# Attention's list schedule: spacings, transposes and exclusions in the planner's costs, and two bias blocks recorded behind the q/k scale's broadcast

## The chip, the cores and the metric

The kernel runs on one core of a Trainium2 chip. The metric is the device time of one execution in microseconds (us). The engines are TensorE (PE, with its weight loads as PEld), VectorE (DVE), ScalarE (ACT), GpSimd (POOL) and SyncE (SP), whose queue issues the DMAs.

## What is computed

An attention with a learned relative bias, whose output is the input of a mixture of experts with a Sinkhorn gate:

```python
# q, k, v: 4 x 8 heads x 576 x 64
scores = q @ k.T / 8
x = log1p(|i - j|) / log1p(max(i, 1))           # 576 x 576
bias = relu(x @ w1 + b1) @ w2                    # one plane for each head
attn = softmax(scores + bias)
y = (attn @ v)                                   # 2304 tokens x 512
P = exp(y @ w_gate - max); 8 times: rows / sum, columns / sum, * N / E
out = sum over 8 experts of P[:, e] * (relu(y @ w1[e]) @ w2[e])     # 512 -> 1024 -> 512
```

## The kernel before, in words

The program has two parts, and each is written to one `Plan`: the code records instructions with an engine, a cost in us, the regions that they read and write, and a priority, and `emit` then orders them. This change concerns the first part, attention, which in the profiled execution takes the first 490 us.

**Attention.** There are 16 units (a batch and a pair of heads). A unit has five steps: two query groups for each head with two tiles of 128 queries each, and one step with a single tile. A step takes for each tile: score matmuls on PE into a PSUM tile (`s`, two buffers), one fused DVE instruction that adds the bias and finds the row's extreme (`sb`, the custom instruction), an exponential with its sum on ACT (in place in `sb`), a scaled copy to 16 bits on ACT (`ah`, high part), and a DVE instruction for the low part. One DMA transpose per step then brings `ah` (18 blocks of 128x128, or 9 for a single tile) into `aT`, and two steps later `attend` multiplies it with the values (28 matmuls into `pv`), after which ACT and DVE split `pv` into two 16-bit parts in the buffers `xa`, `xb`, `xc`. `ah` has two buffers, and a third in `xc` for a part of the units. Besides, each unit has loads of q, k, v and bias, a split of q and k into 16-bit parts (`u_cut`), 18 PE transposes (`u_trans`) and some copies on POOL (`pairs`). PE fills its free time with pieces of expert 0 (`run_piece`, recorded with the lowest priority), whose results go through ACT and POOL.

**Before the first unit** the maxima of q and k are found (loads of 576 KB, one reduction each on DVE or ACT), and their bias is built in 41 blocks. `bias_step` number i records `bias_front(i)` (four matmuls into PSUM tiles `pv`, `l1`, `l2`, `l1`, a Sign on ACT behind each, and the load of a later block's input) and `bias_back(i-1)` (34 or fewer matmuls into `s`, and two or three DVE instructions). The tag `l2` has one PSUM buffer, and the broadcast of the q/k maximum (`bcast_max`: a transpose on PE, a reduction, a diagonal, a matmul, a copy) uses the same buffer twice. Its result `s_qk` is what `u_cut(0)` waits for; bias blocks from number 18 on need the scale as well.

**The order.** `emit` simulates the engines: each has a time at which it is free, each recorded instruction a time at which its inputs are ready (the end of the producer plus `LATENCY` of the pair of engines), and each engine takes at its turn the ready instruction of the lowest priority number and, within one, of the lowest record number; an instruction of priority 0 that is about to be ready holds others back. DMAs go through one pipe (`moved`). The instructions are then emitted in the order of their simulated starts, so what reaches the chip is an order per engine, and waits of an engine in that order hold up all that stands behind. Costs come from `Engine.cost` and `Engine.transfer`, which look at sizes and memory spaces. The second part (gate, Sinkhorn, experts) has costs written beside each instruction; it shares the table `LATENCY` alone.

Old costs of the lines concerned: an exponential over 576 columns is put at 0.16 + 0.03 + 576 x 0.00097 + 0.28 us (the last term for `accum_out`), a transpose DMA at 0.65 us on SP and 2.97 us in the pipe for 18 blocks.

Of the kernel before, what the change touches and what calls it, by code (L numbers as in the profile page):

```python
# [10 lines left out]
F32 = mybir.dt.float32  # L11
# [4 lines left out]
PSUM = bass.MemoryType.PSUM  # L16
DRAM = bass.MemoryType.DRAM

P = 128
# [16 lines left out]
SK = 3.0  # L36
PC = 1.305
MXP = 2
K_VEC = (1, 4, 7)
TM16 = 2.0**-16  # L40
TINY = 2.0**-100


class Plan:
# [1 line left out]


    LATENCY = {
        ("act", "act"): 0.13,
        ("dve", "dve"): 0.13,  # L50
        ("pool", "pool"): 0.1,
        ("pe", "pe"): 0.0,
        ("sp", "sp"): 0.0,
        ("dve", "pe"): 0.26,
        ("pe", "act"): 0.2,
        ("pe", "dve"): 0.2,
    }

    def record(self, eng, cost, fn, ins, outs, move=None):
# [71 lines left out]
    def emit(self):  # L131
        n = self.nodes
        succ, left, ready = [[] for _ in n], [len(x[3]) for x in n], [0.0] * len(n)
        for i, x in enumerate(n):
            for d in x[3]:
                succ[d].append(i)
        avail = {}
        for i, x in enumerate(n):
            if not left[i]:
                avail.setdefault(x[0], []).append(i)  # L140
        free, order, moved = {}, [], 0.0
        key = lambda i: (n[i][4], i)

        def pick(e):

            l = avail[e]
            t = max(free.get(e, 0.0), min(ready[i] for i in l))
            for i in sorted((i for i in l if ready[i] <= t), key=key):
                if not any(n[j][4] == 0 and n[i][4] and t < ready[j] < t + n[i][1] - 0.25 for j in l):
                    return t, e, i  # L150
            t = min(ready[j] for j in l if ready[j] > t)
            return t, e, min((i for i in l if ready[i] <= t), key=key)

        while any(avail.values()):
            t, e, i = min(pick(e) for e in avail if avail[e])
            avail[e].remove(i)
            order.append((t, i))
            free[e] = end = t + n[i][1]
            if n[i][6]:
                moved = max(moved, end + 0.65) + n[i][6][0]  # L160
                end = moved + 0.8
                if e == "dma":
                    free[e] = max(free[e], moved - n[i][6][1])
            for j in succ[i]:
                left[j] -= 1
                ready[j] = max(ready[j], end + n[i][5] + self.LATENCY.get((e, n[j][0]), 0.17))
                if not left[j]:
                    avail.setdefault(n[j][0], []).append(j)
        assert len(order) == len(n)
        for _, i in sorted(order):  # L170
            n[i][2]()
        self.__init__()
# [17 lines left out]
class Engine:  # L190
# [5 lines left out]
    def __getattr__(self, op):  # L196
        def call(*args, **kw):
            outs = [kw[k] for k in ("out", "accum_out") if k in kw]
            rest = list(args)
            if "out" not in kw:  # L200
                outs.insert(0, rest.pop(0))
            ins = [x for x in rest + [v for k, v in kw.items() if k not in ("out", "accum_out")] if isinstance(x, AP)]
            if op == "matmul" and not kw["start"]:
                ins.append(outs[0])
            fn = getattr(self.real, op)
            move = None
            if op.startswith("dma"):
                cost, *move = self.transfer(op, outs[0], ins[0])
            else:
                cost = self.cost(op, outs[0], ins) + (0.28 if self.name == "act" and len(outs) > 1 else 0.0)  # L210
            self.plan.record(self.name, cost, lambda: fn(*args, **kw), ins, outs, move)  # L211

        return call

    def transfer(self, op, out, src):

        if op == "dma_start_transpose":
            return 0.65, 0.165 * out.free_size() / P, 0.92
        run = 1
        for step, n in reversed(list((src if src.space == DRAM else out).ap)):  # L220
            if step != run:
                break
            run *= n
        slow = 2.0 if run * mybir.dt.size(out.dtype) < 512 else 1.0
        return 1.05 if self.name == "pool" else 0.5, out.nbytes() / 275e3 * slow, 1.25

    def cost(self, op, out, ins):

        n = max(x.free_size() for x in [out] + ins)
        columns = sum(x.free_size() == 1 for x in ins)  # L230
        if self.name == "pe":
            c = 4 if ins[0].dtype == F32 else 1
            if out.partition_size() > 64:
                return c * max(64, out.free_size()) / 2350
            return c * max(82, out.free_size()) / 3500
        if self.name == "act":
            return (0.13 if ins and ins[0].space == PSUM else 0.16) + 0.03 * columns + n * 0.00097
        if self.name == "pool":
            return 0.15 + n * (0.0016 if len(ins) - columns < 2 else 0.0021)
        if op == "tensor_copy" and ins[0].dtype == out.dtype == F16:  # L240
            return 0.06 + n * 0.00027
        if n <= 2:
            return 0.08
        return 0.12 + n * (0.0012 if ins[0].space != PSUM else 0.00112)


class Places:
# [24 lines left out]
def attention_sinkhorn_moe(ctx, tc, q, k, v, w1, b1, w2, wg, m1, m2, xm, xm4, xf, sel, out):  # L272
# [12 lines left out]
    vec, act, pool, pe, sync = (  # L285
        Engine(plan, e, n)
        for e, n in ((nc.vector, "dve"), (nc.scalar, "act"), (nc.gpsimd, "pool"), (nc.tensor, "pe"), (nc.sync, "dma"))
    )
# [126 lines left out]
    with ExitStack() as actx:  # L415
# [108 lines left out]
        for kind in range(1, 4):  # L524
            vec.scalar_tensor_tensor(
                out=wr,
# [101 lines left out]
        def bias_step(between=()):  # L628

            i = bpos[0]  # L630
            bpos[0] += 1
            if between:
                if 0 < i <= NBLK:
                    bias_back(i - 1)
                for j, fn in enumerate(between):
                    fn()
                    if j == 0 and i < NBLK:
                        bias_front(i)
                return
            if i < NBLK:  # L640
                bias_front(i)
            if 0 < i <= NBLK:
                bias_back(i - 1)
# [153 lines left out]
        for n in range(8):  # L797
            for m in (2 * n, 2 * n + 1):
                nm, _, i = qk_order[m]
                some_max(mq8[:, int(nm == "k"), i : i + 1], mxt.pop((nm, i)), nm == "k" and i not in K_VEC)  # L800
                if m + 4 < 16:
                    max_load(*qk_order[m + 4])
                elif m + 4 == 16:
                    u_load(0)
                if m + 4 >= 16:
                    max_load("v", v, m - 12)
            bias_step()
            bias_step()
        with plan.urgent():
            mqk = sm([P, 2])  # L810
            vec.tensor_reduce(out=mqk, in_=mq8, axis=AX.X, op=ALU.max)
# [12 lines left out]
            out=g, in0=g0, scalar=s_qk[:, 0:1], in1=s_qk[:, 1:2], op0=ALU.mult, op1=ALU.mult  # L824
        )
        gbox[0] = g[:, 0:1]
        bias_step()

        def b_scale(hp):

# [21 lines left out]
            u_trans(0)  # L852
        u_load(1)
        u_cut(1)
        bias_step()
        b_scale(0)
        u_trans(1)

# [1142 lines left out]
```

## Time and profile before

| what | value |
|---|---|
| median of 3 runs | 1739.29 us (1737.27 to 1740.19) |
| the profiled execution's own time | 1741.8 us |
| its span, first to last instruction | 1740.0 us |
| PE, DVE, ACT, POOL busy | 1666.5, 1437.2, 1057.8, 149.3 us |
| TensorE clock granted, mean | 0.986 of full speed |

The profile is of one execution. Busy time is the union of an engine's instructions; a share of the whole span mixes the attention part, where all engines work, with the expert part, where PE does nearly all of it. The two parts are therefore read in stretches of their own.

### The profile page before, as it was taken

The numbers are of one execution on the slowest core, as the hardware profiler recorded it, in microseconds if no ns is written. First come the engines' busy times: TensorE is split into PE (matmuls) and PEld (weight loads), VectorE is DVE, ScalarE is ACT, GpSimd is POOL, SyncE is SP. The second block draws the span as 40 slices with busy tenths as digits, with TensorE's granted clock in tenths as the row PEclk, the third lists the DMA queues.
The fourth block names the chain that finished last, engine by engine and source line by source line (L and its number), as shares of the span: only waits on it lengthen the run. The fifth ranks groups of instructions, "written<-read, shape, count | busy, mean of one in ns | idle before, by whom it ended". The sixth has DMA issues, their size and how long they took to land.

```text
span 1740.0 us, 40362 instructions
## 1 busy us (share of the span) xinstructions
PE 1666.5 (96%) x16596; PEld 1367.8 (79%) x16596; DVE 1437.2 (83%) x2595; ACT 1057.8 (61%) x1879; POOL 149.3 (9%) x191
## 2 busy tenths in 40 slices
PE   7887897999999999999999999999999999999998
PEld 4554564656585888888988898889888888888887
DVE  7998999889769999687878887988788878876666
ACT  7887888888857555456455545555555644443443
POOL 0102231323212300000000000000000000000000
PEclk9988898999999999999999999999999999999999
DMA  7869999999875446644664555456544743462321
GB/s 256 257 174 233 186 205 216 212 213 213 177 239 200 158 161 239 232 150 143 217 231 170 176 190 209 176 178 238 203 165 159 279 157 131 183 225 97 102 75 37
DMA packets 291964, 324.60 MB, mean 187 GB/s; under 512 B 183100, under 2 KB 217412, under 8 KB 286788
## 3 DMA queue, kind: packets, MB, share of 16 engines
q1 hardware_dynamic: 291780, 322.04, 61.6%
q8 instruction: 129, 2.11, 0.5%
q14 instruction: 55, 0.45, 0.1%
HBM read 191.43 MB, written 88.08 MB: 161 GB/s over the span
## 4 chain that ended last, share of the span: by engine, by line
PE 76%; DVE 5%; DMA 2%; ACT 1%; issue 1%; POOL 0%; DVEq 0%; SPq 0%; ACTq 0%; POOLq 0%
PE bankA L1612 18%; PE bankA L1632 14%; PE bankE L1632 9%; PE bankB L1632 9%; PE bankE L1612 9%; PE l L211 6%; PE bankB L1612 4%; PE pv L211 3%; PE s L211 2%; DMA aT<-ah 1%; PE bankB L375 1%; DVE c L1224 1%; DMA xb<-in_moe_w_dram 1%; PE bankE L375 1%; DVE ah L211 0%
## 5 line engine op out<-in xcount | busy, mean ns | idle before, releaser
L1612 PEld LDWEIGHTS <-slot 128*128 128x128 f16 x5040 | 451.0, 98 | 52.2 <-issue 6.4
L1632 PEld LDWEIGHTS <-hA 128*128 128x128 f16 x2268 | 221.0, 98 | 26.6 <-DVE hA L1224 1.2
L211 PEld LDWEIGHTS <-area 128*128 128x128 f16 (+1 forms) x2477 | 153.6, 100 | 101.3 <-issue 31.7
L1612 PE MATMUL bankA<-xt,slot 128*128 128x256 f16 (+1 forms) x1680 | 186.1, 262 | 1.4 <-ACT u L1669 1.4
L1612 PE MATMUL bankE<-xt,slot 128*128 128x256 f16 (+1 forms) x1680 | 186.1, 262 | 0.3 <-DVE c L1224 0.3
L1657 ACT ACTIVATE hA<-c 128x512 f16<-128x512 f32 x189 | 118.3, 628 | 107.8 <-DVE c L1224 106.8
L1632 PEld LDWEIGHTS <-hS 128*128 128x128 f16 x1512 | 147.6, 98 | 20.2 <-DVE hS L1663 1.9
L1632 PEld LDWEIGHTS <-area 128*128 128x128 f16 x1512 | 147.7, 98 | 17.1
L1716 ACT COPY u<-bankA 128x512 f32<-128x512 f32 (+1 forms) x70 | 38.0, 542 | 181.3 <-PE bankA L1632 181.2
L1224 DVE SCALAR_TENSOR_TENSOR hA<-c,hA 128x512 f16<-128x512 f32 x189 | 128.4, 691 | 15.9 <-ACT hA L1657 13.9
L1669 ACT ACTIVATE u<-bankA 128x512 f32<-128x512 f32 x126 | 75.2, 597 | 79.0 <-PE bankA L1612 72.2
L211 ACT ACTIVATE sb<-sb,st 128x576 f32<-128x576 f32 x144 | 110.5, 769 | 8.7 <-DVE st L211 8.5
L211 PE MATMUL l<-area 128*128 128x512 f16 (+1 forms) x413 | 110.6, 384 | 4.7 <-ACT area L211 1.3
L211 DVE SCALAR_TENSOR_TENSOR ah<-sb,st,ah 128x576 f16<-128x576 f32 x121 | 101.8, 869 | 13.4 <-ACT ah L211 12.9
L1224 DVE SCALAR_TENSOR_TENSOR acc<-c,fs,acc 128x256 f32<-128x256 f32 x252 | 110.3, 479 | 2.1
L211 ACT ACTIVATE ah<-sb,st 128x576 f16<-128x576 f32 x121 | 88.5, 770 | 19.3 <-DMA aT<-ah 14.4
L211 PE MATMUL s<-qkT 128*128 128x512 f16 (+3 forms) x560 | 82.7, 296 | 16.1 <-DVE st L211 14.7
L1632 PE MATMUL bankA<-area,hS 128*128 128x256 f16 x756 | 88.9, 273 | 1.8 <-ACT hS L1657 1.0
L1632 PE MATMUL bankA<-area,hA 128*128 128x256 f16 x756 | 88.4, 273 | 1.0 <-DVE hA L1224 1.0
L1632 PE MATMUL bankB<-area,hA 128*128 128x256 f16 x756 | 88.3, 273 | 0.0
L1632 PE MATMUL bankB<-area 128*128 128x256 f16 x756 | 88.3, 273 | 0.0
L1632 PE MATMUL bankA<-area 128*128 128x256 f16 x756 | 88.3, 273 | 0.0
(248 smaller groups left out, 3192.2 us busy)
## 6 DMA issues: line engine op xcount, KB each, us to landing
sc_w<-stage SPq DMA_DIRECT2D x84, 512.0 KB
acc<-sc_y SPq DMA_DIRECT2D x102, 256.0 KB
area<-sc_w SPq DMA_DIRECT2D x48, 512.0 KB
sc_y<-acc SPq DMA_DIRECT2D x84, 256.0 KB
xt<-sc_t SPq DMA_DIRECT2D x20, 1024.0 KB
slot<-sc_w SPq DMA_DIRECT2D x36, 512.0 KB
bt<-sc_bias SPq DMA_DIRECT2D x26, 576.0 KB
raw<-in_moe_w_dram SPq DMA_DIRECT2D x28, 512.0 KB
```

Source lines behind the costliest of these rows:

```text
L211: self.plan.record(self.name, cost, lambda: fn(*args, **kw), ins, outs, move)
L375: pe.matmul(ps, w[:, a, ft * P : (ft + 1) * P], xs(xp, dt, p0, W), start=(dt == 0 and j == 0), stop=(dt == 3 and j == 2),)
L1224: vec.scalar_tensor_tensor(out=o, in0=x, scalar=s, in1=y, op0=op0, op1=op1)
L1612: pe.matmul(ps[:, jf * w : jf * w + w], t[:, a, c * 512 + f * P : c * 512 + f * P + P], x(xp, c), start=(first and jf == 0 and c == 0 and ...
L1632: pe.matmul(ps[:, j * 256 : j * 256 + 256], h[:, a, fc * w + j * P : fc * w + j * P + P], t[:, wp, fc * 256 : fc * 256 + 256], start=(firs ...
L1657: on_act(0.58, lambda: act.activation(h[:, 0, sl], x, AF.Relu if relu else AF.Copy), [r], wk)
L1669: on_act(0.55, lambda: act.activation(tmp[k], bank[b], f, scale=HS), [b], [k], 0)
L1716: on_act(0.27 * nt, lambda: act.copy(tmp[k][:, :n], bank[b][:, :n]), [b], [k], 0)
```

## The change

`LATENCY`, the costs of all engines, the handling of DMAs and the simulation of transposes are replaced; a rule is added that POOL instructions and DVE instructions with several SBUF inputs (or with one, where copies and `tensor_scalar` are concerned) don't run at once; and the two `bias_step`s that the last round of the maxima recorded (numbers 15 and 16) are recorded after the q/k scale. The next two follow `u_cut(1)`, where before one stood ahead of `u_cut(0)` and one behind `u_cut(1)`. What is computed, and the instructions themselves, stay.

```diff
+EARLY = 2
+PEC = 1.08
     LATENCY = {
-        ("act", "act"): 0.13,
-        ("dve", "dve"): 0.13,
-        ("pool", "pool"): 0.1,
+        ("act", "act"): 0.055,
+        ("act", "dve"): 0.225,
+        ("act", "pe"): 0.225,
+        ("dve", "dve"): 0.06,
+        ("dve", "act"): 0.2,
+        ("dve", "pe"): 0.2,
+        ("pool", "pool"): 0.0,
+        ("pool", "dve"): 0.12,
+        ("pool", "pe"): 0.12,
         ("pe", "pe"): 0.0,
+        ("pe", "act"): 0.29,
+        ("pe", "dve"): 0.29,
         ("sp", "sp"): 0.0,
-        ("dve", "pe"): 0.26,
-        ("pe", "act"): 0.2,
-        ("pe", "dve"): 0.2,
     }
...
             order.append((t, i))
+            if e == "pool" or n[i][6] == "shared":
+                t = max(t, free.get(("shared", e != "pool"), 0.0))
+                free["shared", e == "pool"] = t + n[i][1]
             free[e] = end = t + n[i][1]
-            if n[i][6]:
-                moved = max(moved, end + 0.65) + n[i][6][0]
-                end = moved + 0.8
-                if e == "dma":
-                    free[e] = max(free[e], moved - n[i][6][1])
+            if n[i][6] and n[i][6] != "shared":
+                if not n[i][6][0]:
+                    free[e] = end = max(end, moved - 0.2 + n[i][1])
+                moved = max(moved, end + 0.5) + n[i][6][0]
+                end = moved + 0.75
+                free[e] = max(free[e], moved - n[i][6][0] - n[i][6][1]) if n[i][6][0] else free[e]
...
+            big = [x for x in ins if x.free_size() > 1]
+            if self.name == "dve" and not any(x.space == PSUM for x in big):
+                one = len(big) == 1 and op in ("tensor_scalar", "tensor_copy", "tensor_single_scalar")
+                move = "shared" if len(big) > 1 or one and outs[0].free_size() > 1 else None
...
-                cost = self.cost(op, outs[0], ins) + (0.28 if self.name == "act" and len(outs) > 1 else 0.0)
+                cost = self.cost(op, outs[0], ins) + (0.093 if self.name == "act" and len(outs) > 1 else 0.0)
...
         if op == "dma_start_transpose":
-            return 0.65, 0.165 * out.free_size() / P, 0.92
+            return 0.149 * out.free_size() / P + 0.06, 0.0, 0.0
...
-        return 1.05 if self.name == "pool" else 0.5, out.nbytes() / 275e3 * slow, 1.25
+        return 0.5, out.nbytes() / 300e3 * slow, 1.5
...
         if self.name == "pe":
-            c = 4 if ins[0].dtype == F32 else 1
-            if out.partition_size() > 64:
-                return c * max(64, out.free_size()) / 2350
-            return c * max(82, out.free_size()) / 3500
+            c = (4 if ins[0].dtype == F32 else 1) * max(64, out.free_size()) / 2375
+            return PEC * (c if out.partition_size() > 64 else c / 2)
         if self.name == "act":
-            return (0.13 if ins and ins[0].space == PSUM else 0.16) + 0.03 * columns + n * 0.00097
+            return (0.052 if psum else 0.186) + n * 0.00083
         if self.name == "pool":
-            return 0.15 + n * (0.0016 if len(ins) - columns < 2 else 0.0021)
+            return 0.08 + n * (0.00115 if len(full) < 2 else 0.0025)
+        if op == "tensor_tensor_reduce":
+            return 0.735
+        if n <= 2:
+            return 0.183 if op.startswith("tensor_s") else 0.165 if op == "tensor_copy" else 0.09
         if op == "tensor_copy" and ins[0].dtype == out.dtype == F16:
-            return 0.06 + n * 0.00027
-        if n <= 2:
-            return 0.08
-        return 0.12 + n * (0.0012 if ins[0].space != PSUM else 0.00112)
+            return 0.6 if psum else 0.16 + n * 0.00027
+        if op == "tensor_scalar" and not psum:
+            return 0.12 + n * 0.00054
+        return 0.065 + n * 0.00106 + (0.055 if len(full) > 1 and op == "scalar_tensor_tensor" else 0.0)
...
-            bias_step()
-            bias_step()
+            if n < 7:
+                bias_step()
+                bias_step()
         with plan.urgent():
             mqk = sm([P, 2])
...
         gbox[0] = g[:, 0:1]
-        bias_step()
+        for _ in range(EARLY):
+            bias_step()
...
         u_cut(1)
-        bias_step()
+        for _ in range(4 - EARLY):
+            bias_step()
         b_scale(0)
```

## Rows read from the trace of the kernel before

**Rows 1.** Stretches: us, busy PE PEld DVE ACT POOL (count), clock, DMA share, GB/s

```profile
60.00:150.00 90.00, 78.32 (x1079) 48.45 (x1076) 83.80 (x167) 80.89 (x160) 15.76 (x27) 0.94 0.74 196
150.00:300.00 150.00, 122.45 (x1188) 75.99 (x1187) 138.39 (x312) 120.60 (x238) 35.21 (x47) 0.91 0.97 211
300.00:450.00 150.00, 143.32 (x1452) 93.80 (x1453) 131.98 (x299) 125.43 (x256) 44.85 (x58) 0.98 1.05 215
...
700.00:1740.00 1040.00, 1031.45 (x9908) 926.46 (x9905) 819.15 (x1339) 530.98 (x877) 0.00 (x0) 1.00 0.49 171
```

**Rows 2.** Timeline, all engines, near 490: start us, us, engine, line, what

```profile
490.81 1.36 PE L1280 MATMUL bankS<-wgs,xa 128*128 128x8 f16 x48
```

**Rows 3.** Groups by form, 0 to 490: names, shapes, count | busy us, mean ns

```profile
L211 ACT ACTIVATE sb<-sb,st 128x576 f32<-128x576 f32 x144 | 110.5, 769 | 8.7 <-DVE st L211 8.5
...
L211 ACT ACTIVATE area<-l 128x512 f16<-128x512 f32 x120 | 65.0, 625 | 4.4 <-PE l L211 4.2
```

**Rows 4.** Timeline, ACT and DVE: starts of like instructions one behind the other

```profile
53.65 1.57 ACT L211 ACTIVATE area<-l 128x512 f16<-128x512 f32 x3
...
307.43 0.76 ACT L211 ACTIVATE sb<-sb,st 128x576 f32<-128x576 f32 x1
...
308.18 0.77 ACT L211 ACTIVATE sb<-sb,st 128x576 f32<-128x576 f32 x1
...
311.76 0.81 DVE L211 CUSTOM_DVE_ANT_0 sb<-s,bt,sms 128x576 f32<-128x576 f32 x1
...
312.50 0.81 DVE L211 CUSTOM_DVE_ANT_0 sb<-s,bt,sms 128x576 f32<-128x576 f32 x1
```

**Rows 5.** Who waited for whom, 0 to 490: us in total, times, longest us

```profile
PE s L211 <- DVE st L211: 17.9, 18, 3.0
...
ACT ah L211 <- DMA aT<-ah: 14.4, 13, 2.6
DVE ah L211 <- ACT ah L211: 12.9, 13, 2.6
DVE sb L211 <- PE s L211: 11.8, 16, 1.9
...
DVE xc L211 <- ACT xc L211: 5.9, 3, 4.5
DVE aT L211 <- PE s L211: 5.5, 9, 1.1
...
PE pv L211 <- DMA aT<-ah: 4.2, 5, 1.9
```

**Rows 6.** Timeline, all engines: from the q/k maximum to the first cut

```profile
47.11 0.17 DVE L211 TENSOR_REDUCE sms<-sms 128x2 f32<-128x16 f32 x1
...
48.22 1.73 ACT L211 ACTIVATE area<-l 128x512 f16<-128x512 f32 x3
...
55.24 0.27 PE L211 MATMUL l<-ident,sms 128*2 128x128 f32 x1
...
59.35 1.44 ACT L211 ACTIVATE qk<-nat,sms 128x576 f16<-128x576 f32 x2
```

**Rows 7.** Chain of waits in order of time: start us, us, what

```profile
311.52 1.89 PE pv L211 x28
...
393.57 5.04 DMA aT<-ah
```

**Rows 8.** Timeline, SP's queue: the transpose of the chain above

```profile
393.57 3.10 SPq L211 DMA_TRANSPOSE aT<-ah  x1
```

**Rows 9.** Instructions by tile `aT`: duration ns min/median/max, first and last start us

```profile
L211 SPq DMA_TRANSPOSE aT<-ah x67: 1277/3104/5950, 91.6 to 483.5; - x67
...
L211 SPq DMA_TRANSPOSE aT<-xc x13: 1277/2110/4824, 232.5 to 390.3; - x13
```

**Rows 10.** Timeline, all engines: a POOL copy and a DVE scaling of resident bias

```profile
64.19 1.80 POOL L211 COPY qkT<-qkT 64x576 uint32<-64x576 uint32 x2 [61.66 <-ACT qkT L211]
64.20 1.26 DVE L211 TENSOR_SCALAR br<-br,sms 128x1152 f32<-128x1152 f32 x1
```

More of the change, by code (lines that the diff above doesn't have):

```diff
@@ L224, in transfer @@
         slow = 2.0 if run * mybir.dt.size(out.dtype) < 512 else 1.0
-        return 1.05 if self.name == "pool" else 0.5, out.nbytes() / 275e3 * slow, 1.25
+        return 0.5, out.nbytes() / 300e3 * slow, 1.5
     def cost(self, op, out, ins):
         n = max(x.free_size() for x in [out] + ins)
-        columns = sum(x.free_size() == 1 for x in ins)
+        full = [x for x in ins if x.free_size() > 1]
+        psum = any(x.space == PSUM for x in full)
         if self.name == "pe":
-            c = 4 if ins[0].dtype == F32 else 1
-            if out.partition_size() > 64:
-                return c * max(64, out.free_size()) / 2350
-            return c * max(82, out.free_size()) / 3500
+            c = (4 if ins[0].dtype == F32 else 1) * max(64, out.free_size()) / 2375
+            return PEC * (c if out.partition_size() > 64 else c / 2)
         if self.name == "act":
-            return (0.13 if ins and ins[0].space == PSUM else 0.16) + 0.03 * columns + n * 0.00097
+            return (0.052 if psum else 0.186) + n * 0.00083
         if self.name == "pool":
-            return 0.15 + n * (0.0016 if len(ins) - columns < 2 else 0.0021)
+            return 0.08 + n * (0.00115 if len(full) < 2 else 0.0025)
[3 more added lines that the diff above has]
+            return 0.183 if op.startswith("tensor_s") else 0.165 if op == "tensor_copy" else 0.09
         if op == "tensor_copy" and ins[0].dtype == out.dtype == F16:
-            return 0.06 + n * 0.00027
-        if n <= 2:
-            return 0.08
-        return 0.12 + n * (0.0012 if ins[0].space != PSUM else 0.00112)
+            return 0.6 if psum else 0.16 + n * 0.00027
+        if op == "tensor_scalar" and not psum:
+            return 0.12 + n * 0.00054
+        return 0.065 + n * 0.00106 + (0.055 if len(full) > 1 and op == "scalar_tensor_tensor" else 0.0)
 class Places:
```

## The prediction

> **What bounds the kernel now.** I read the busy times by stretch first, because the change can only move the order of instructions, and order is worth something only where engines stand idle. The expert part has nothing to give: from 700 to the end PE is busy 1031.45 of 1040 us, 8.6 us idle [rows 1]. Attention ends when the gate's first matmuls start, at 490.81 [rows 2]. Inside it no single engine is the bound. From 60 to 150 DVE is idle 90 - 83.80 = 6.2 us and ACT 9.1; from 150 to 300 DVE 11.6 and PE 27.6; from 300 to 450 PE only 6.7, DVE 18.0, with the DMA share at 1.05 [rows 1]. So DVE leads before 300, PE and the DMA queue after. What idle time there is comes from in-order engines that stand before an instruction not yet ready while others behind it are; the reader finds these in the view of who waited for whom, and they are what a truer plan can shrink.
>
> Next I compared what the planner believes with the starts in the timeline. An exponential starts 308.18 - 307.43 = 0.75 us after the one before [rows 4]; the old plan says 0.16 + 0.03 + 576 x 0.00097 + 0.28 = 1.03, the new 0.186 + 576 x 0.00083 + 0.093 = 0.757. Three Signs take 1.57 us [rows 4], and one alone 0.625 [rows 3], so (1.57 - 0.625) / 2 = 0.47 each; old 0.627, new 0.477. With 144 exponentials and 120 such Signs [rows 3] the old plan carries 144 x 0.28 + 120 x 0.155 = 59 us of ACT work that the chip doesn't do: it thinks ACT is the bottleneck and is surprised by an ACT that comes early. The fused DVE instruction has a spacing of 312.50 - 311.76 = 0.74 [rows 4]; old 0.765, new 0.735, so DVE was known well already.
>
> **The change part by part.** It removes and adds no instruction; its costs are waits.
>
> *ACT's cost.* ACT arrives early at the copy into `ah`, whose buffer is still read by a transpose: 13 waits, 14.4 us, and behind each stands DVE for the low part: 13 waits, 12.9 us [rows 5]. A plan that knows ACT's speed puts other ACT work there. But the same change makes the landing optimistic. In the trace a transpose lands 5.04 us after its issue [rows 7], whose row in the queue is 3.10 long [rows 8]: 1.94 us behind the row's end. The old plan has 0.65 + 0.65 + 2.97 + 0.80 = 5.07 from the issue, right to 0.03; the new one has 18 x 0.149 + 0.06 = 2.74 in the queue and 0.5 + 0.75 = 1.25 behind it, 0.7 us short of 1.94. If each of the 13 waits keeps 0.7 us, 9.1 of the 14.4 stay and 5.3 go, 37%; of DVE's 12.9 that is 4.7 us. Bounds: all 12.9 gone, or 0.7 us more for each (+9.1).
>
> On completion the Trainium skill (DMA: Bandwidth & Descriptors, section Anatomy of one DMA — SWDGE (gpsimd) path) puts a fixed cost of about 2.0 us on a DMA, most of it the confirmed arrival of the last byte; it says so of DMAs issued from GpSimd, and the 1.94 us here, from SP, agree with it. By its figure the new plan would be 0.75 us short instead of 0.7, and 13 x 0.05 = 0.65 us more of ACT's waits would stay. It speaks against the new constant; the rival with a slower time is its result.
>
> *PE's hand-offs.* DVE waits 11.8 us in 16 places for scores, PE 17.9 us in 18 places for a free score buffer [rows 5]. Costs on both sides were near the trace; latencies are changed by under 0.1 us (0.2 to 0.29 from PE, 0.26 to 0.2 from DVE). These waits come mostly from drift between engines, of which ACT's error is the largest; I take a third of DVE's, 4 us. Bounds: 0, and all 11.8. The waits of DVE for scores in the bias blocks (5.5 us in 9 places [rows 5]) are shorter each; I take 1 us, between 0 and 5.5.
>
> *The values' product.* 28 matmuls take 1.89 us [rows 7]; the old plan has 28 x 256 / 3500 = 2.05, the new 28 x 1.08 x 256 / 2375 / 2 = 1.63. It is now 0.26 us too short where it was 0.16 too long, so ACT and DVE will stand a little earlier before `pv`: DVE's 5.9 us behind that [rows 5] stay as they are, 0 for the sum (gone: -5.9; longer by 0.26 for each of 3: +0.8). PE's own waits for a landing are 4.2 us in 5 places [rows 5]; 0.7 us more in each is 3.5. Expert 0's pieces can't step in once PE stands, but in 150 to 300 PE has idle time anyway; a third reaches the end, +1.2 (0 to 3.5).
>
> *Exclusion of POOL and DVE.* A scaling of resident bias that starts beside a POOL copy takes 1.26 us [rows 10], where the new cost is 0.12 + 1152 x 0.00054 = 0.74. The new rule makes the plan wait, it doesn't choose another instruction for that reason. It moves the simulated times nearer to the chip's and nothing else: 0, at best the 0.52 us for each of the 8 scalings (-4), at worst as much.
>
> *SP.* 80 transposes (67 and 13 [rows 9]) hold SP's queue 2.74 us each in the plan, where the old one blocked it for about 0.65 + 0.65 + 2.97 - 0.92 = 3.35; the trace's middle is 3.10 for the larger group. Loads may be issued earlier by that; they queue behind the same transposes, so 0. Bounds from the excess of 1.05 over a full share [rows 1]: 5% of 150 us, 7.5 us, either way.
>
> *Two bias blocks.* The maximum is reduced at 47.11, yet the broadcast's transpose starts at 55.24 [rows 6], 0.02 us after the Signs of 53.65 to 55.22 have freed the one `l2` buffer [rows 4]. These belong to block 16, the last recorded ahead of the broadcast. Now block 14's are the last, which end at 48.22 + 1.73 = 49.95 [rows 6]: the broadcast and the first cut come 5.3 us earlier, the cut near 54 instead of 59.35. Each moved block brings 4 matmuls, 4 Signs, an input load on SP of 72 KB, and 34 matmuls with two DVE instructions; on SP it goes behind loads for v and the second unit. Little is won, for the first softmax step also needs the resident bias whole, blocks up to 17, and DVE is 93% busy in 60 to 150 [rows 1]. I take -1; if the cut let ACT fill as much as its idle share there (9.1 of 90, 10% of 5.3 us on each side and the same on DVE), about -2; if the late blocks hold the first step, +2.
>
> *The second part* uses the latencies. PE's order there follows priorities and record numbers, and it is 99% busy: 0, between -2 and +4 (half its 8.6 us of idle time doubled).
>
> Sum: -4.7 - 4 - 1 + 1.2 - 1 = -9.5 us, all of it inside the first 490. Against the profiled execution (1741.8, span 1740.0, 1.8 us around it) that is 1732.3; that execution lies 2.5 us above the median of the runs, 1739.3, so the forecast is 1729.8.
>
> **The rivals.** *No free DMA time.* If the queue of transposes and loads is what sets the pace from 150 to 450, DVE waits for `ah` whatever the plan says. For: share 0.97 and 1.05 [rows 1], and transposes of up to 5.95 us against 3.10 in the middle [rows 9]. Against: a share above 1 counts packets that wait as well as those that move. About two thirds of the three gains fall there (300 of 430 us): 9.7 x 2/3 = 6.5 are lost, leaving -9.5 + 6.5 = -3, 1736.3. That the order hardly changes, since dependences fix most of it, gives the same to -0: together 1736 to 1741.
>
> *The early landing.* The plan issues `attend` and the next `ah` copies 0.7 us before they can start, and this happens at most transposes and not at the 18 that wait today. Each of the 16 units has 3 products. With 48 that stand 0.7 us each on PE, half of it covered by PE's idle time, 48 x 0.35 = 17 us are added and the 9.5 of the forecast kept: 1747. The point: over 9.5 / 0.35 = 27 such products eat the gain. For: 5.07 against 3.99 planned, 5.04 measured. Against: a product is due two steps after its transpose, so most are ready long before.
>
> *A better fit than I count.* Half of all four DVE waits named (12.9 + 11.8 + 5.9 + 5.5 = 36.1), 18 us, and 2 for the bias blocks: 1719.
>
> **How the numbers follow.** Forecast 0.50 (1723 to 1735.5), the better fit 0.10, no effect 0.19, the early landing 0.21. A measurement of this kernel tells about 0.2%, 3.5 us, from no change. Faster: 0.50 + 0.10 less 0.01 for the edge, 0.59; within: 0.20; slower: 0.21. The range goes from 1718, which takes in the better fit, to 1745, which takes in some half of the slower cases; about 0.13 is left out. The unknown bounds (SP 7.5, second part +4) lie inside it.
>
> **What would show it.** The broadcast's transpose at about 50 instead of 55.24; gate matmuls at about 481; ACT's waits for `aT` down to about 9 us, not to none; DVE's waits behind them down with them; PE's waits for `aT` a little up. Wrong would be: attention ending near 490 with the DMA share unchanged (the first rival), PE's waits for landings of 15 us or more (the second), or a change behind 700, which I count as none.

## The result: 13 us slower, and the profile after

The changed kernel takes 1751.77 us in the median (1750.86 to 1752.47) beside 1738.74 (1737.27 to 1740.55) for the kernel before on the same chip: a ratio of 1.0076, 95% interval 1.0064 to 1.0087, so 13.0 us slower. The forecast was 1729.8 and its range ended at 1745. The profiled execution took 1752.47 us with a span of 1750.7; the mean granted clock is 0.986 in both profiles, so it explains nothing of the loss.

The stretches of after (length, then busy us of PE, PEld, DVE, ACT and POOL with their counts, the clock, the DMA share, GB/s), to be laid beside [rows 1]:

```profile
60.00:150.00 90.00, 77.42 (x1061) 47.83 (x1060) 84.05 (x166) 77.76 (x156) 14.21 (x23) 0.92 0.78 199
150.00:300.00 150.00, 120.07 (x1201) 75.16 (x1200) 138.13 (x316) 123.39 (x246) 40.50 (x49) 0.93 0.94 208
300.00:450.00 150.00, 140.62 (x1405) 91.30 (x1404) 129.89 (x286) 121.70 (x247) 48.24 (x58) 0.98 0.99 209
700.00:1750.70 1050.70, 1035.80 (x9941) 929.71 (x9939) 825.82 (x1349) 535.34 (x888) 0.69 (x1) 1.00 0.49 172
```

Two things are seen. From 300 to 450 PE, DVE and ACT are all less busy than before: PE's idle time goes from 6.7 to 9.4 us and DVE's from 18.0 to 20.1. And behind 700, where I had counted on nothing, PE's idle time goes from 8.6 to 1050.70 - 1035.80 = 14.9 us.

The gate's first matmuls, where attention ends, in PE's timeline of after (start, length, engine, line, operation); before they started at 490.81 [rows 2]:

```profile
497.82 1.35 PE L1301 MATMUL bankS<-wgs,xa 128*128 128x8 f16 x48
```

Attention ends 7.0 us later, and from there to the end it is 1750.7 - 497.82 = 1252.9 us instead of 1740.0 - 490.81 = 1249.2: 3.7 more in this pair of executions (the timed medians put it higher, below).

Its beginning went as foretold. After's timeline has, in place of [rows 6]:

```profile
47.14 0.17 DVE L226 TENSOR_REDUCE sms<-sms 128x2 f32<-128x16 f32 x1
49.57 0.27 PE L226 MATMUL l<-ident,sms 128*2 128x128 f32 x1
51.72 1.44 ACT L226 ACTIVATE qk<-nat,sms 128x576 f16<-128x576 f32 x2
65.29 0.81 DVE L226 CUSTOM_DVE_ANT_0 sb<-s,br,sms 128x576 f32<-128x576 f32 x1
```

The broadcast's transpose starts at 49.57 instead of 55.24, the first cut at 51.72 instead of 59.35, the first fused instruction at 65.29 instead of 67.98. The first transpose DMA starts at 83.4 us instead of 91.6, but the second at 97.17 beside 97.64; from the third on the lead lies between -0.2 and 6.2 us. At the 40th of the 80 the lead is 309.2 - 306.4 = 2.8 us; by the one at 331.0 (before 328.5) it is gone; the last starts at 488.1 instead of 483.5. So in this pair the loss in attention is made between 300 and 490, not at the blocks that moved. The row of these transposes in after, to be laid beside [rows 9]:

```profile
L226 SPq DMA_TRANSPOSE aT<-ah x67: 1280/2764/5833, 83.4 to 488.1; - x67
```

Who waited for whom, 0 to 510, in after (total us, times, longest), beside [rows 5]:

```profile
DVE ah L226 <- ACT ah L226: 26.7, 24, 3.3
ACT sb L226 <- DVE st L226: 17.2, 23, 2.7
ACT ah L226 <- DMA aT<-ah: 14.9, 10, 3.2
PE s L226 <- DVE st L226: 14.4, 18, 1.9
DVE xc L226 <- ACT xc L226: 10.5, 8, 6.8
PE pv L226 <- DMA aT<-ah: 9.6, 8, 2.0
DVE sb L226 <- PE s L226: 3.6, 8, 1.1
```

The waits changed places. DVE's for scores fell from 11.8 to 3.6 us, as the forecast wanted, and PE's for a free score buffer from 17.9 to 14.4. ACT's for a landing, foretold at about 9, stayed at 14.9 (before 14.4). But DVE's for ACT's high part, which should have fallen from 12.9 to 8.2, rose to 26.7; PE's for a landing rose from 4.2 to 9.6; and ACT's for DVE, a row that I hadn't weighed, doubled. In the profile of before it was:

```profile
ACT sb L211 <- DVE st L211: 8.5, 11, 1.7
```

### The profile page after: what moved, and what is told of

It is laid out like the page before. It is cut to its first block, busy times and chain, and to the rows that moved or that the text cites. A ratio compares the mean times of both kernels' runs of the same rounds, so it can differ in the third digit from the quotient of the medians.

```text
span 1750.7 us, 40347 instructions
## 1 busy us (share of the span) xinstructions
PE 1664.1 (95%) x16596; PEld 1365.2 (78%) x16596; DVE 1439.1 (82%) x2595; ACT 1054.7 (60%) x1879; POOL 152.4 (9%) x191
## 4 chain that ended last, share of the span: by engine, by line
PE 70%; DVE 4%; DMA 2%; ACT 1%; issue 1%; POOL 0%; ACTq 0%; DVEq 0%; SPq 0%; POOLq 0%
PE bankA L1633 18%; PE bankA L1653 14%; PE bankE L1653 9%; PE bankB L1653 9%; PE bankE L1633 9%; PE bankB L1633 4%; PE l L226 2%; DMA aT<-ah 2%; PE pv L226 1%; PE bankB L393 1%; PE bankE L393 1%; DVE c L1245 1%; PE s L226 1%; DMA sc_w<-stage 0%; ACT u L1690 0%
## 5 line engine op out<-in xcount | busy, mean ns | idle before, releaser
L226 DVE SCALAR_TENSOR_TENSOR ah<-sb,st,ah 128x576 f16<-128x576 f32 x121 | 109.0, 929 | 27.2 <-ACT ah L226 26.7
L226 ACT ACTIVATE ah<-sb,st 128x576 f16<-128x576 f32 x121 | 88.4, 768 | 18.1 <-DMA aT<-ah 14.9
L1653 PE MATMUL bankE<-area,hS 128*128 128x256 f16 x756 | 88.5, 273 | 1.5 <-ACT hS L1678 1.1
```

The costliest lines, as they stand in the source:

```text
L1653: pe.matmul(ps[:, j * 256 : j * 256 + 256], h[:, a, fc * w + j * P : fc * w + j * P + P], t[:, wp, fc * 256 : fc * 256 + 256], start=(firs ...
```

## Experiments

First theory (mine): the loss is the early landing in attention; the rest of the new costs helps. First rival: the order of the second part, through `LATENCY`, loses it. Second rival: no single constant does it; the list's order scatters with any of them.

All results, so that the kernels can be laid side by side. "Difference" is the median less the median of the kernel before on the same chip (its interval is given as a ratio). "Gate" is the start of the gate's first matmuls in that kernel's profile, "rest" its span less that.

| kernel | median us | difference | ratio, 95% | gate | rest |
|---|---|---|---|---|---|
| before | 1738.74 | | | 490.81 | 1249.2 |
| after | 1751.77 | +13.0 | 1.0064 to 1.0087 | 497.82 | 1252.9 |
| e1: before, blocks moved | 1740.59 | +1.0 | 0.9996 to 1.0017 | 489.12 | 1248.0 |
| e2: after, blocks not moved | 1746.19 | +6.6 | 1.0033 to 1.0063 | 488.78 | 1254.0 |
| e3: after, landing 1.45 | 1745.99 | +6.4 | 1.0026 to 1.0056 | 487.39 | 1256.8 |
| e4: after, experts by the old table | 1746.46 | +6.9 | 1.0026 to 1.0056 | 496.01 | 1249.1 |
| e5: after, PEC 1.07 | 1744.04 | +3.9 | 1.0009 to 1.0030 | 486.63 | 1256.3 |
| e6: after, PEC 1.09 | 1745.15 | +5.0 | 1.0027 to 1.0051 | 485.37 | 1255.3 |
| e7: after, landing 1.10 | 1746.30 | +6.1 | 1.0019 to 1.0046 | 491.17 | 1254.2 |
| e8: e2 and the old table for experts | 1740.73 | +0.5 | 0.9995 to 1.0015 | 491.51 | 1247.3 |
| e9: e5 and the old table for experts | 1737.05 | -2.8 | 0.9973 to 0.9994 | 484.42 | 1249.3 |
| e10: before, experts from PE 0.29 | 1740.62 | +0.7 | 0.9992 to 1.0017 | 491.52 | 1247.5 |
| e11: before, experts' four ways from ACT, DVE | 1752.68 | +12.8 | 1.0048 to 1.0090 | 490.64 | 1262.8 |
| e12: before without 26 bias loads | 1737.80 | -2.1 | 0.9976 to 1.0001 | 486.70 | 1248.9 |
| e13: e9 with PEC 1.075 | 1743.07 | +2.7 | 1.0009 to 1.0030 | 494.19 | 1247.1 |
| e14: e9 with PEC 1.085 | 1738.41 | -2.0 | 0.9976 to 0.9998 | 485.31 | 1247.3 |
| e15: before, experts ACT to PE 0.225 | 1739.71 | -0.7 | 0.9983 to 1.0005 | 487.57 | 1250.3 |
| e16: before, experts ACT and DVE, both ways | 1743.96 | +3.6 | 1.0008 to 1.0031 | 491.43 | 1253.8 |
| e17: e9 with PEC 1.09 | 1741.24 | +0.3 | 0.9984 to 1.0013 | 492.44 | 1247.1 |
| e18: before, experts DVE to PE 0.20 | 1739.67 | -1.3 | 0.9982 to 1.0002 | 489.49 | 1250.7 |

### The change taken apart: blocks, plan, landing, experts

e1 is before with the new places of the `bias_step`s, e2 is after with the old ones:

```diff
-            bias_step()
-            bias_step()
+            if n < 7:
+                bias_step()
+                bias_step()
...
-        bias_step()
+        for _ in range(EARLY):
+            bias_step()
...
```

> The kernel before with the two bias blocks recorded behind the q/k scale, the planner's costs as before. If the move does what the trace of the change suggests (its first transpose starts at 83.4 us instead of 91.6, its tenth 2.3 us earlier), this kernel is at 1735 to 1738 us, 1 to 4 us under before, and the gate's matmuls start at 487 to 490. Rival: the early gain comes from the new costs, or is given back later by an order that falls out differently; then 1738 to 1743.

> The changed kernel with the bias blocks recorded where they were before: the new planner's costs and latencies alone. If the whole loss is the planner's, and the blocks gave 1 to 4 us, it is at 1753 to 1756 us. Rival: the moved blocks cost something too; then it is under 1751.

e3 gives transposes the landing that the trace has, e4 keeps the new table for attention and orders the second part with the old one:

```diff
-                end = moved + 0.75
+                end = moved + (0.75 if n[i][6][0] else 1.45)
```

```diff
+    plan.LATENCY = {("act", "act"): 0.13, ("dve", "dve"): 0.13, ("pool", "pool"): 0.1, ("pe", "pe"): 0.0, ("sp", "sp"): 0.0, ("dve", "pe"): 0.26, ("pe", "act"): 0.2, ("pe", "dve"): 0.2}
     plan.emit()
```

> The changed kernel with one number altered: a transpose's data are taken to be there 1.45 us behind the model's transfer instead of 0.75, so 1.95 us behind the end of its row, as the traces show (1.94 and 1.98 in the middle). Theory of the early landing: ACT's waits for aT (14.9 us), DVE's for ACT behind them (26.7) and PE's for aT (12.5 with xc) fall to half or less, and the gate's matmuls start 5 to 9 us earlier than in the changed kernel (497.8): 1743 to 1747 us. Rival (another part of the costs, or mere scatter of the list's order, makes the loss of attention): waits and start within 3 us of the changed kernel's, 1749 to 1755.

> The changed kernel with the old latencies while the second part (gate, Sinkhorn, experts) is put in order; attention as changed. Theory: the latencies cost the second part 4 to 6 us (from the gate's first matmul to the end 1249.2 us before, 1252.9 in the changed kernel, and PE idle 14.9 instead of 8.6 us from 700 on); then this kernel is at 1746 to 1748, with 1248 to 1250 us from the gate's start. Rival: the second part is late because attention hands it something late (buffers, the order of loads); then 1751 to 1753 and 1252 to 1254 us.

The blocks alone make no difference that can be measured. Each of the other three takes about half of the loss away, and in two different halves: e2 and e3 bring the gate back (488.78, 487.39) and keep the long rest (1254.0, 1256.8); e4 keeps the late gate (496.01) and has the rest of before (1249.1). So there are two losses, and the first theory can hold for one of them at most. The gates are single profiles, but the medians divide in the same way once e8 and e9, below, are laid beside e2 and e5.

### Attention: is it the landing?

e7 puts the landing half way, at 1.10 where e3 has 1.45. e5 and e6 leave the landing at 0.75 and change something that should not matter, the factor on PE's costs, by 1%. e8 is e2 with e4's table: the whole plan, in attention alone, without the moved blocks.

```diff
-PEC = 1.08
+PEC = 1.07
```

> The changed kernel with the landing of transposes at 1.1 us behind the model's transfer, halfway between 0.75 (gate at 497.8) and 1.45 (487.4). Theory of the early landing: a start in between, 490 to 495, with DVE's waits behind ACT's ah between 26.7 and 18.8 us. Scatter: no order in it; under 488 or over 497 as likely as between.

> The changed kernel with PEC at 1.07 instead of 1.08: a change of 1% in the planned cost of matmuls, which by itself is worth nothing. If the late landing in the plan is the cause of attention's loss, the gate's matmuls start at 494 to 500 us as in the changed kernel (497.8, and 496.0 with the same attention in the run with the old latencies for the experts), and 1749 to 1754 us result. If the loss is scatter of the list's order (bias blocks alone 489.1, plan alone 488.8, both 497.8, both with the longer landing 487.4), the start moves by 3 us or more, to 486 to 493, and the time with it: 1741 to 1748.

> The same with PEC at 1.09. Landing: gate at 494 to 500, 1749 to 1754 us. Scatter: anywhere from 486 to 500, and not where the run with 1.07 lies.

> The new planner for attention, the bias blocks where they were, the old latencies for the experts. If the parts add up (plan alone 1746.2; old latencies took 5.3 us off the changed kernel), it is at 1740 to 1742 us, the same as before. If the plan alone makes attention better (488.8 against 490.8) and nothing else is lost, 1736 to 1739.

All of them end attention at 485 to 492. A landing that is 0.7 us early, with PE's costs 1% up or down, shows no loss in attention's end; nor does it in e8, whose median was +0.5. In e8 the waits for landings are even below before's (ACT 7.5 us, PE 3.9):

```profile
ACT sb L226 <- DVE st L226: 18.8, 16, 2.9
PE s L226 <- DVE st L226: 15.1, 18, 1.6
DVE ah L226 <- ACT ah L226: 14.0, 21, 2.4
DVE sb L226 <- PE s L226: 13.3, 13, 2.2
ACT ah L226 <- DMA aT<-ah: 7.5, 7, 2.0
PE pv L226 <- DMA aT<-ah: 3.9, 4, 1.6
```

So the early landing is not the cause by itself. To see what the plan is worth apart from scatter, e9, e13, e14 and e17 run PEC 1.07, 1.075, 1.085 and 1.09 with the old table for the experts; e4 is the point 1.08.

> The changed kernel with PEC 1.07 for attention and the old latencies for the experts. If the two losses are separate and add, 1744.0 less 5.4 us (5.3 and 5.5 in the two pairs run so far) gives 1738 to 1740 us, not to be told from before; from the gate's first matmul less idle time of PE in the last part, 8 instead of 13 us. If the better attention order gives something beside, 1735 to 1737.

> The changed kernel with PEC 1.075 and the old latencies for the experts; beside it stand 1.08 (1746.5 us, gate's start 496.0) and 1.07 (1737.1, 484.4). If the planned cost of matmuls matters in itself, this lies between them, 1740 to 1744 and a start of 488 to 493. If 1.08 happens to give a bad order among others of like quality (scatter), this lies with the neighbours, 1735 to 1741 and 484 to 491, or is off on its own.

> The same with PEC 1.085. A cost that matters in itself: 1746 or more, start 495 to 500, though 1.09 (start 485.4) already speaks against it. Scatter: 1735 to 1742, start 484 to 492.

> The changed kernel with PEC 1.09 and the old latencies for the experts, the fifth point beside 1.07 (1737.1 us), 1.075 (1743.1), 1.08 (1746.5) and 1.085 (1738.4). With the new latencies 1.09 was at 1745.2, so 5.4 less gives 1738 to 1741 if the two parts add. If the scan has a trend after all, 1745 or more.

In the order of PEC the differences to before are -2.8, +2.7, +6.9, -2.0 and +0.3: no trend, neighbours 2 to 9 us apart, mean (-2.8 + 2.7 + 6.9 - 2.0 + 0.3) / 5 = +1.0. The forecast's gain of 9.5 is at none of the five points. Even e9, the fastest kernel here that computes everything (1737.05, 0.17% under before), mostly exchanges waits. Its executions, like those of e14, also show a higher granted clock than those of before on the same chips (0.988 and 0.989 in the mean beside 0.985); whether their 2 to 3 us come from the order itself or from that wasn't tried. The rows of e9, 0 to 490:

```profile
ACT sb L226 <- DVE st L226: 22.6, 29, 2.5
DVE ah L226 <- ACT ah L226: 19.8, 21, 2.5
PE pv L226 <- DMA aT<-ah: 8.9, 7, 2.6
ACT ah L226 <- DMA aT<-ah: 6.9, 8, 2.1
DVE sb L226 <- PE s L226: 6.4, 7, 1.9
```

ACT's waits for landings fell to 6.9 us here, below the 9 that was foretold, and DVE's at `ah` rose all the same. DVE's two waits, for ACT's high part and for scores, add up to 24.7 us before, 24.1 in e14, 26.2 in e9, 27.3 in e8, 29.5 in e13, 30.2 in e17 and 30.4 in e4; the times go 0, -2.0, -2.8, +0.5, +2.7, +0.3 and +6.9. So much of what helps DVE for scores is paid back at `ah`, but e17, with 30.2 and no loss, shows that this sum alone doesn't set the time.

What sets the worst order apart in the traces is the low part's DVE instruction, the one that waits at `ah`: 929 ns in the mean in after and in e4, the two kernels with that order, 895 in e13 (+2.7), 845 to 868 in e2, e3, e5, e6, e8, e9, e14 and e17, and 864 to 881 with old costs. e7 is the exception: 901, and no more than the experts' share of loss. All 24 of after's 121 that take more than 1 us run beside a POOL instruction, and so do the 12 of before; the 68 that have none beside them take 795 to 820 ns. A pair from after:

```profile
411.19 0.82 DVE L226 SCALAR_TENSOR_TENSOR ah<-sb,st,ah 128x576 f16<-128x576 f32 x1 [1.52 <-ACT ah L226]
412.56 1.54 POOL L226 TENSOR_TENSOR area<-ys,area 128x512 f16<-128x512 f32 x1
413.01 1.71 DVE L226 SCALAR_TENSOR_TENSOR ah<-sb,st,ah 128x576 f16<-128x576 f32 x1
```

After has 49 of them with POOL beside them for more than a fifth of their time, before 27; e2, e3, e5, e8 and e9 have 39 or 40, at 956 to 979 ns in the mean against after's 1099. No run moves POOL's instructions alone, so that this is the cause of the loss isn't shown.

### Attention: is it the DMA queue?

e12 takes out of the kernel before all 26 loads of bias tiles (576 KB each) of the units that load them, and lets these units use the resident bias of tile 0, so that their scores carry another tile's bias:

```diff
-            bt = bst.tile([P, 2, S], F32, name="bt", tag="bt")
-            sync.dma_start(out=bt, in_=sc_bias[2 * units[u][1] + hh])
-            U[u]["b", hh] = bt
+            U[u]["b", hh] = br[0][:, 0:2, :]
```

> The kernel before without the 26 loads of bias for query tiles 2 and 3 (576 KB each, 15.3 MB); these tiles read the resident bias of tile 0 instead, so their scores differ from the reference's. DVE, ACT and PE do what they did. If attention goes at the pace of the DMA queue, 15.3 MB at the 215 GB/s of the steady stretch are 71 us of it, and the gate's matmuls start 12 us or more before 490.8. If not (engines in order, with the waits shared among them), the start stays within 487 to 494.

Windows and gate of e12 (columns as above):

```profile
150.00:300.00 150.00, 123.18 (x1203) 76.38 (x1203) 139.64 (x316) 123.00 (x244) 34.24 (x47) 0.91 0.81 172
300.00:450.00 150.00, 144.92 (x1473) 94.72 (x1470) 133.32 (x304) 125.49 (x259) 48.44 (x63) 0.99 0.84 166
```

```profile
486.70 1.36 PE L1278 MATMUL bankS<-wgs,xa 128*128 128x8 f16 x48
```

The DMA share falls from 0.97 to 0.81 and from 1.05 to 0.84, 15.3 MB are gone, and attention ends 4.1 us earlier than in the profile of before, the kernel 2.1 with an interval that touches no change. At the pace of the queue 12 us or more were expected. So the loads in the queue don't set the pace; the transposes stayed in it, and of them alone this says nothing.

### The experts: which latency?

The table's rest splits cleanly. Nine profiles whose second part was ordered by the old table (before, e1, e4, e8, e9, e12, e13, e14, e17) have a rest of 1247.1 to 1249.3 us, six with the new one (after, e2, e3, e5, e6, e7) 1252.9 to 1256.8. In timed medians four pairs differ by this table alone: after and e4 6.1 us, e2 and e8 6.1, e5 and e9 6.7, e6 and e17 4.7 (differences of their differences), 5.9 in the mean. To find the entry, before was given parts of the new table for the second part alone. The fences show lines of the table set for the second part beside the old one. e10:

```diff
-            ("pe", "act"): 0.2,
-            ("pe", "dve"): 0.2,
+            ("pe", "act"): 0.29,
+            ("pe", "dve"): 0.29,
```

e11 has these four entries, e16 the first two of them, e15 the third alone and e18 the fourth alone:

```diff
+            ("act", "dve"): 0.225,
+            ("dve", "act"): 0.2,
+            ("act", "pe"): 0.225,
-            ("dve", "pe"): 0.26,
+            ("dve", "pe"): 0.2,
```

> The kernel before, with two latencies altered while the experts are put in order: from PE to ACT and to DVE 0.29 instead of 0.2. In the changed kernel PE waits in the experts at about ten places 0.73 us for ACT's copy of a bank, where the product S4 follows S1 in the same bank and A22's product, which before stands between them, comes later. If the longer way from PE makes A22 late in the plan, this kernel shows most of the 5 us: 1743 to 1746 and PE idle 11 to 14 us in the last part. Rival (the ways from ACT and DVE do it): 1738 to 1741, idle 8 us.

> The kernel before, experts ordered with the new latencies between ACT, DVE and to PE (0.225, 0.225, 0.2, 0.2), those from PE and within an engine old. The counterpart of the run before: 1743 to 1746 if these ways make A22 late, 1738 to 1741 if they do not. If neither run shows the 5 us, it takes both.

> The kernel before, experts ordered with one altered latency: from ACT to PE 0.225 instead of 0.17. If PE's operands written by ACT alone are what comes late in the plan, it shows the loss of the run with all ways from ACT and DVE (1752.7): 1746 or more. Otherwise as before, 1738 to 1742.

> The kernel before, experts ordered with the latencies between ACT and DVE altered alone: 0.225 and 0.2 instead of 0.17 and 0.17. A22's operand goes bank, ACT, DVE, ACT, DVE before PE reads it, so these two ways count up to three times in it. If they make it late in the plan: 1745 to 1754 us, with PE idle 12 us or more in the last part and waits for ACT's copy of a bank. Otherwise 1738 to 1742.

> The kernel before, experts ordered with one altered latency: from DVE to PE 0.2 instead of 0.26. The pair between ACT and DVE costs 3.6 us, all ways from ACT and DVE together 12.8, the way from ACT to PE nothing. If the way from DVE to PE is worth the difference by itself, 1746 or more; if it only adds up with the pair, 1738 to 1742.

Nothing that can be measured from PE's ways, from ACT to PE or from DVE to PE (rests of 1247.5 to 1250.7); 3.6 us from the pair between ACT and DVE; 12.8 from all four together. The profile shows where. PE's waits in the second part, first of before, then of after, of e16 and of e11 (the rows that differ):

```profile
PE bankA L1612 <- ACT u L1669: 2.9, 5, 0.7
```

```profile
PE bankA L1633 <- ACT u L1690: 7.4, 10, 0.7
PE bankE L1653 <- ACT hS L1678: 1.1, 1, 1.1
```

```profile
PE bankA L1612 <- ACT u L1669: 9.6, 13, 0.7
```

```profile
PE bankA L1612 <- ACT u L1669: 9.7, 13, 0.7
PE bankE L1632 <- ACT hS L1657: 4.7, 1, 4.7
```

And one such wait in after's timeline (what is in brackets: idle time before it, and what ended it):

```profile
794.09 1.47 PE L1633 MATMUL bankA<-xa,area 128*128 128x256 f16 x12
795.65 0.60 ACT L1690 ACTIVATE u<-bankA 128x512 f32<-128x512 f32 x1 [0.73 <-PE bankA L1633]
796.30 1.47 PE L1633 MATMUL bankA<-xc,slot 128*128 128x256 f16 x12 [0.73 <-ACT u L1690]
```

PE finishes a product of 12 matmuls in `bankA` and the next in its order is another for the same bank: it stands 0.73 us until ACT has copied the bank out. (The trace leaves buffer numbers out: `bankA` stands for two banks, and here both products are for the same one.) Before, at such a place, products of the second layer (L1632) follow the same product:

```profile
788.11 1.47 PE L1612 MATMUL bankA<-xa,area 128*128 128x256 f16 x12
789.41 2.78 PE L1632 MATMUL bankE<-area,hA 128*128 128x256 f16 x24
792.03 2.78 PE L1632 MATMUL bankA<-area,hA 128*128 128x256 f16 x24
```

The second-layer product in `bankE` has an operand (`hA`) that goes from the bank to ACT, DVE, ACT and DVE again. With longer planned ways between these two (0.225 and 0.2, where the old table had no entry and the list takes 0.17) it is ready later in the plan, and PE's order takes the next block's first product, for the same bank, instead. Counted in the kernels' instruction orders, with the two banks told apart, a block's last first-layer product is directly followed by such a one 3 times in before and in e10, 13 times in e16 and in e11, and 11 times in after. On the chip the operand mostly is there in time: with before's order PE stands for 8.6 us in all behind 700. For after these rows add 7.4 - 2.9 + 1.1 = 5.6 us, and PE's idle time behind 700 grew by 14.9 - 8.6 = 6.3, beside the 5.9 of the pairs. For e16 they add 6.7, where the timing has 3.6. For e11 they add 6.8 + 4.7 = 11.5 beside 12.8; why the four entries together also bring the one wait of 4.7 us, which neither the pair nor a single entry brings, wasn't settled. The whole new table costs 5.9 and its four ways alone 12.8, so its other entries (within an engine, and from PE and POOL) give some of that back when they come together; no run tries them so.

## Why the prediction was wrong, step by step

- *The second part, "0, between -2 and +4".* The first failed step. It measured +5.9 (4.7 to 6.7), above its bound. My reason was that PE's order there follows priorities and record numbers and that PE is 99% busy. Both rows were right; but a PE that is 99% busy has no cover, so a place where the order falls the wrong way can cost up to its 0.73 us, and which products are ready when the list picks them hangs on latencies. I had read the idle time (8.6 us [rows 1]) as the size of the risk. It is the size of the possible gain only.
- *ACT's true cost, -4.7, and PE's hand-offs, -4 and -1.* The second failed step. In after, with the experts' part taken out (e4), attention brings +6.9; over five neighbouring plans +1.0 in the mean, and never -9.7. The planner's error was real, and the waits that I gave to PE's hand-offs did fall in after (11.8 to 3.6; 3.6 to 13.3 over the runs with the new plan). The 13 waits of DVE that I took to stand behind ACT's 13 for a landing don't move with them: in e9 ACT's are 6.9 us and DVE's 19.8, in e2 6.2 and 12.8. But I let a wait that goes become time, and did not say what is late next: with DVE, PE and ACT all 80 to 95% busy from 150 to 450 (after's stretches above), DVE stands a little later at `ah` for what it no longer stands at `sb`. The prediction took a third or more of each wait as gain from the share that it would shrink, with no row that shows a shorter wait making an earlier end.
- *The product of the values (0) and landing on PE (+1.2).* PE's waits for landings rose by 5.4 us in after (4.2 to 9.6), more than the bound of 3.5, but not in e8 (3.9), e3 (4.4) or e14 (3.6), two of which have the same landing of 0.75. The size comes with the order, not with the constant.
- *Exclusion, 0.* The low part's DVE instruction takes 929 ns in the mean in after, where the page of before has 869 for the same line:

```profile
L211 DVE SCALAR_TENSOR_TENSOR ah<-sb,st,ah 128x576 f16<-128x576 f32 x121 | 101.8, 869 | 13.4 <-ACT ah L211 12.9
L226 DVE SCALAR_TENSOR_TENSOR ah<-sb,st,ah 128x576 f16<-128x576 f32 x121 | 109.0, 929 | 27.2 <-ACT ah L226 26.7
```

  That is 7.2 us more of DVE's time under a plan that keeps these instructions and POOL's apart; on the chip more of them met (49 of 121 instead of 27). In e8, with the same rule, it is 866 ns, so neither the gain of 4 nor a loss belongs to the rule; it moves with the order. My bounds, 4 us either way, looked at the 8 scalings and left out the 121 low parts, where a meeting costs up to 0.9 us.
- *SP, 0.* After's DMA share is lower from 150 on (0.94 and 0.99), and e12 shows that even 0.2 less of it is worth at most a few us. Right, as far as it shows.
- *Two bias blocks, -1 (between -2 and +2).* The mechanism came as told, and e1 shows it by itself (about 50 and near 54 were foretold):

```profile
49.52 0.27 PE L212 MATMUL l<-ident,sms 128*2 128x128 f32 x1
54.30 1.44 ACT L212 ACTIVATE qk<-nat,sms 128x576 f16<-128x576 f32 x2
```

  The gain did not: e1 measured +1.0, interval -0.7 to +3.0, no difference. The earlier cut doesn't reach the first transpose DMA, which starts at 91.8 us in e1 and 91.6 before; with the new costs alone (e2) it starts at 89.9, and only with both at 83.4. That DVE, 93% busy from 60 to 150, is what eats the 5 us is likely but not shown.
- *The rival "No free DMA time"* falls by e12 as far as the loads go. Its time, 1736.3 to 1741, is where most plans of attention without the experts' part land (e9 1737.05, e14 1738.41, e8 1740.73, e17 1741.24; not e13 and e4). The other reason that it named, that the order hardly changes, isn't it: the waits show that the orders differ, and they gain nothing to speak of.
- *The rival "The early landing"* had the right sign, and that 1747 is near e4's 1746.46 is luck as far as the runs show: e5, e6 and e8 keep the early landing and lose nothing in attention, and PE's waits for landings were 12.5 us in after (9.6, and 2.9 for `xc`), under the 15 that were to show it. Waits of ACT and PE (with its weight loads) for the landings of `ah` are 25.4 us in after, 20.1 before, and 10.8 to 19.2 in e2, e3, e7, e8, e9, e13 and e14, but 24.8 in e17, which loses nothing. The landing itself is as read: 1.98 us behind the end of the row in the middle of after's transposes, 1.94 before, where the new plan has 1.25. The Trainium skill (DMA: Bandwidth & Descriptors, section Anatomy of one DMA — SWDGE (gpsimd) path) has about 2.0 us for the fixed part of a DMA issued from GpSimd, and the trace agrees with it for transposes issued from SP. But that a constant is wrong doesn't say what it costs: mending it (e3) gave the same as moving PEC by 1% (e5, e6). Why the order at PEC 1.08 with moved blocks is worse than its neighbours by 4 to 9 us stays open; its meetings of low part and POOL are the nearest trace of a cause.
- *Chances and range.* The two failed terms are separate (the table takes 4.7 to 6.7 us off with four different orders of attention), and the one in attention could go either way. A plan whose neighbours lie 9 us apart needs a range of about that width on each side for attention alone, and one more term for the experts; mine left out 0.13.

## What to carry to other kernels

When a change alters the costs of a list scheduler, it draws a new order, and the spread between neighbouring draws (here 9.7 us between PEC 1.08 and 1.07) is the first term of the forecast; measure it with two or three harmless changes of a constant before you believe that a better model gives a better order. A constant that is shared with another part of the program re-orders that part too, and a part whose engine is 99% busy can gain little by it and lose more: keep the tables apart, as e9 and e14 do, which are the versions to use (0.1 to 0.2% under before, the best two of five drawn). And a shorter wait is time only if you can name the engine that is then no longer late; where three engines are busy at 80 to 95%, assume that it comes back as another wait.

## What the runs showed of the hardware that was not expected

- One order of attention doesn't have one time. e6 and e17 have the same instruction order there, and their gates start at 485.37 and 492.44, 7.1 us apart. With before's order (before, e10, e11, e15, e16, e18) the gate starts between 487.57 and 491.52. A single profile therefore can't tell a gain of 5 us in attention; the timed medians can.
- The granted clock differs between executions of one kernel, and the time with it. Over the 117 executions of before that were timed beside the experiments the median is 1742.1 us at a mean clock of 0.983 (12 executions), 1740.4 at 0.985 (34) and 1738.7 at 0.986 (34). One place where it differs is in e17, where the clock is 0.50 from 355 to 360, the lower of its two levels (1.2 and 2.4 GHz), after PE was busy for 2.67 of the 5 us from 350; in e6, with the same order, PE was busy for 2.94 of these 5 us and the clock stays at 1.00. What share of the 7.1 us above that is wasn't tried.
- The same 121 DVE instructions for the low part take 869 ns in the mean before, 929 in after and 866 in e8, with the same work and the same rule on POOL in the latter two: where no POOL instruction runs beside them they take 811 ns in the mean before and 813 in after, and up to 1.72 us where one does. An order moves the durations too, here by 63 ns x 121 = 7.6 us of DVE's time, as much as the loss in attention; that it is the cause there was not tried.
